# Retention with a top-k MLP on one core: decay moved from k to v, v loaded by another queue, masks split over two engines

## The chip, the core and the metric

The kernel runs on one core of a Trainium2 chip. A core has five engines that each work through a list of instructions of their own, in order: TensorE (PE: matrix products and transposes, results in PSUM), VectorE (DVE), ScalarE (ACT), GpSimd (POOL) and SyncE (SP, used here only to start transfers). DMA engines move data between memory and SBUF. Semaphores join the lists. PSUM has eight banks of 2 KB per partition; the kernel keeps one for the state and hands out the other seven.

The metric is the device time of one execution in microseconds (us), median of several. The profile is of one execution; its span is a little shorter than the time.

## The reference, cut to what matters

```python
# q, k, v: (4 batches, 8 heads, 768 positions, 64), float32
gamma = 1.0 - 2.0 ** (-5.0 - np.arange(H))             # one decay per head
state = zeros(B, H, 64, 64)
for t in range(S):
    state = gamma * state + k[:, :, t] (outer) v[:, :, t]
    y[:, :, t] = scale * (q[:, :, t] @ state)          # scale = 1/8
x = y as (B, 768, 512)                                  # heads side by side

for b in range(B):                                      # the second part
    scores = x[b] @ w_gate                              # one number per row
    top = the 128 rows of highest score
    h  = max(x[b, top] @ w1, 0)                         # 512 -> 1024
    ye = h @ w2                                         # 1024 -> 512
    out[b] = x[b];  out[b, top] += sigmoid(scores[top]) * ye
```

The recurrence is computed by chunks of 128 positions. Inside a chunk the output is (scores with a causal mask) times v; what came before is a 64 x 64 state per head. The decay between positions i and j is gamma^(i-j) = gamma^i times gamma^(-j), so one factor can be put on q and the other on k. The factor gamma^(-j) can as well be put on v: each term of the sum is a number (q_i . k_j) times the row v_j, and each term of the state is k_j times the row v_j.

## The kernel before

A block is two chunks (256 positions) of one batch; there are 12 blocks, three per batch. The file describes each step as a task with an engine, a length, a "due" and what it reads and writes. A planner inside the file orders the tasks by these numbers, and the instruction lists follow that order. The planner's numbers steer only the order; nothing waits for them on the chip. Only the parts that matter here are shown.

```python
def load(name, src, dst, t):                 # k, q, v of block t: fp32 in memory, bf16 in SBUF
    def fn(eng):
        nc.gpsimd.dma_start(dst[t]..., ap)   # all 36 loads and 8 weight loads are issued by GpSimd
    P.add(f"L{name}{t}", ("POOL", 0.8), fn, t * 3.0 - 40.0, wr=[(name, t)], dma=1.33)

# per block t
# KS: k times gamma^(-j); on VectorE for the first and last block, else on GpSimd
e.tensor_mul(ks[ring][:, r, hs, :], kx[t][:, hs, r, :], gks...)      # 4 per block, 128x256
# TK/CK: transpose ks (8 matmuls), copy PSUM -> kT (VectorE or ScalarE, in fact 10 and 2 of 12)
# TQ/CQ: transpose q (16 matmuls), qT = PSUM * gamma^i (VectorE)
# QK.j, j = 0, 1: 16 matmuls each, scores of four heads into two banks
def mk(eng, j=j, ar=ar):                     # M: the causal mask, from PSUM, fp32 -> bf16
    nc.vector.tensor_mul(am[ar]..., PS[:, ba[j].at:ba[j].at + 2, :]..., mask...)
# AV.j: am times v (16 matmuls each), QS: state times qT (4 per chunk), summed in bank by[c]
# KV: state += ks x v, 8 matmuls of 128 columns per chunk. A pair of heads shares a 128x128
#     square, of which only the two 64x64 squares on the diagonal are wanted:
def se(eng, c=c, cc=cc):                     # SE: copy only those, two operations per chunk
    for s in range(2):
        nc.scalar.activation(sn[s * 64:(s + 1) * 64, :, s * 64:(s + 1) * 64], PS[...], AF.Copy)
# per chunk: YC: xs = scale * PSUM (ScalarE), SC: scores = sum(PSUM * wg) (VectorE)

# ranking, per chunk c of a batch: RB: turn the score column into a row (matmul with identity),
# SR: copy it to SBUF, CM: compare with all earlier chunks and count (VectorE, width 128*(c+1))
# per batch (select): SP: split scores in three bf16 parts (GpSimd), CS: column sums (matmuls),
# RK, OH: one-hot rows of the 128 selected (VectorE), IG/AX/IX: their row numbers and scores,
# SG: sigmoid
# store_base: xs to out (GpSimd); fetch: gather the 128 rows from out by number
# mlp: XT (transpose), XE (copy), W1 (32 matmuls), RL (relu), W2 (8 matmuls), then
# CB (VectorE): ot = gate * W2 + rows; SS: scatter ot to out by row number (GpSimd)
```

The last batch is treated in another way: the 128 best of its first four chunks are selected, gathered and put through the MLP, and the last two chunks are put through the MLP whole ("dense"). A comparison of scores then zeroes the gate of those rows that are not among the best 128 of all six chunks.

```python
b = B - 1; NE = NC - 2
select(b, NE, e); store_base(b, NE, e - 1.0); fetch(b, e)
...                                          # counts against the scores of chunks 4 and 5
mlp(B - 1, xg[b], [("xg", b)], T1 + 1.0, 1, scatter(B - 1, b, "flc", gfl[:, 2:3]))
dense(0, j4); dense(1, j5)                   # an MLP over each of the last two chunks, plain stores
```

Of the kernel before, what the change touches and what calls it, by code (L numbers as in the profile page):

```python
# [36 lines left out]
class Task:  # L37
    __slots__ = ("name", "engs", "fn", "due", "deps", "users", "allocs", "banks", "n", "left",
                 "start", "end", "eng", "dma", "land", "idx")
# [11 lines left out]
class Plan:  # L51
# [7 lines left out]
    def add(self, name, engs, fn, due, rd=(), wr=(), alloc=(), use=(), dma=None, after=()):  # L59
# [4 lines left out]
        t.dma = dma  # L64
# [22 lines left out]
    def run(self):  # L87
# [10 lines left out]
        dma_at = 0.0  # L98
        lanes = []
# [13 lines left out]
        def place(n):  # L113
            best = None
            rng = range(self.first, self.nbanks - n + 1)
            if n == 1:
                rng = reversed(rng)
            for i in rng:
                if any(bank_held[i:i + n]):
                    continue  # L120
                f = max(bank_free[i:i + n])
                if best is None or f < best[0] - 0.05:
                    best = (f, i)
            return best

        while ready:
            cands = []
            for t in ready:
                got = 0.0
                if t.allocs:  # L130
                    held = sum(not h for h in bank_held)
                    need = sum(b.n for b in t.allocs)
                    if held - need < max(b.reserve for b in t.allocs):
                        continue
                    save_h = list(bank_held)
                    ok = True
                    for b in t.allocs:
# [5 lines left out]
                        for i in range(p[1], p[1] + b.n):  # L143
                            bank_held[i] = True
                    bank_held[:] = save_h
                    if not ok:
                        continue
                for eng, dur in t.engs:
                    s = max(free[eng], got)
                    for d in t.deps:  # L150
                        s = max(s, latency(d, eng))
                    if t.dma and len(lanes) >= 8:
                        s = max(s, lanes[-8])
                    cands.append((s, s + dur, t, eng, dur))
# [25 lines left out]
            if t.dma is not None:  # L180
                dma_at = max(dma_at, e + 0.9) + t.dma
                t.land = dma_at + 1.3
                lanes.append(t.land)
# [16 lines left out]
def kernel(  # L200
# [43 lines left out]
    kx = buf("kx", [128, H, 2, D], BF, NT)  # L244
    qx = buf("qx", [128, H, 2, D], BF, NT)
    vx = buf("vx", [128, H, 2, D], BF, NT)
    ks = buf("ks", [128, 2, H, D], BF, 3)
# [3 lines left out]
    sbd = buf("sbd", [128, HP, 128], BF, 2)  # L251
# [12 lines left out]
    gate = buf("gate", [128, 2], FT, B + 1)  # L264
# [3 lines left out]
    ot = buf("ot", [128, Dm], FT, B + 2)  # L268
    w1 = consts.tile([128, HP, F], BF, name="w1")
    w2 = consts.tile([128, FB, Dm], BF, name="w2")  # L270
    wg = consts.tile([128, Dm], FT, name="wg")
    spacer = consts.tile([1, 1], FT, name="spacer")

    P = Plan(8, 1)
    TAU = 4.6

    def load(name, src, dst, t):
        b, blk = divmod(t, NBK)
        ap = bass.AP(tensor=src.tensor, offset=src.offset + b * H * S * D + blk * 2 * C * D,
                     ap=[[2 * D, 128], [S * D, H], [1, 2 * D]])  # L280

        def fn(eng):
            nc.gpsimd.dma_start(dst[t].rearrange("p h r d -> p h (r d)"), ap)  # L283
        return P.add(f"L{name}{t}", ("POOL", 0.8), fn, t * 3.0 - 40.0, wr=[(name, t)], dma=1.33)
# [9 lines left out]
    thr = consts.tile([128, 1], FT, name="thr")  # L294
# [7 lines left out]
    gks = consts.tile([128, H, NBK * 2], FT, name="gks")  # L302

    load("k", k, kx, 0)
# [6 lines left out]
    load("q", q, qx, 0)  # L311
# [7 lines left out]
    load("v", v, vx, 0)  # L319
# [6 lines left out]
    P.add("lg", ("DVE", 0.6), c_lg, -50, wr=["lg", "ones1"])  # L326
# [5 lines left out]
    def c_gks(eng):  # L332
        for h in range(H):
            nc.scalar.activation(gks[:, h, :], pos.rearrange("p b r -> p (b r)"), AF.Exp, bias=0.0,
                                 scale=-lgam[h])
# [23 lines left out]
    def c_sbd(eng):  # L359
        for i in range(2):  # L360
            nc.vector.memset(sbd[i], 0.0)
    P.add("sbd0", ("DVE", 0.6), c_sbd, -2, wr=[("sbd", 0), ("sbd", 1)])

# [7 lines left out]
    def c_late(eng):  # L371
        nc.gpsimd.iota(slotf, pattern=[[1, 128]], base=0, channel_multiplier=0,
                       allow_small_or_imprecise_dtypes=True)
        nc.gpsimd.iota(thr, pattern=[[0, 1]], base=128, channel_multiplier=-1,
                       allow_small_or_imprecise_dtypes=True)
        nc.gpsimd.iota(tokf, pattern=[[0, 1]], base=0, channel_multiplier=2,
                       allow_small_or_imprecise_dtypes=True)
    P.add("late", ("POOL", 0.8), c_late, 9.0, wr=["slotf", "thr", "tokf"])

    def c_late2(eng):  # L380
        nc.gpsimd.tensor_copy(slots, slotf)
        nc.gpsimd.tensor_scalar(tokf[64:128], tokf[64:128], -127.0, None, op0=OP.add)
        for j in range(NCH):
            nc.gpsimd.memset(aux[:, j:j + 1, 0], float(C * j))
        nc.gpsimd.tensor_copy(aux[:, :, 1], tokf.to_broadcast([128, NCH]))
    P.add("late2", ("POOL", 3.0), c_late2, 12.0, rd=["slotf"], wr=["slots", "tokf"]
# [7 lines left out]
    for t in range(1, 3):  # L394
        load("k", k, kx, t)
        load("q", q, qx, t)
        load("v", v, vx, t)
    gq_part(1)
    gq_part(2)
    for t in range(3, NT):  # L400
        load("k", k, kx, t)
        load("q", q, qx, t)
        load("v", v, vx, t)

    def load_w(i):
        def fn(eng):
            if i < 4:
                nc.gpsimd.dma_start(w1[:, :, i * 256:(i + 1) * 256],
                                    bass.AP(tensor=moe_w1.tensor, offset=moe_w1.offset + i * 256,
                                            ap=[[F, 128], [128 * F, HP], [1, 256]]))  # L410
            else:
                f = 2 * (i - 4)
                nc.gpsimd.dma_start(w2[:, f:f + 2, :],
                                    bass.AP(tensor=moe_w2.tensor, offset=moe_w2.offset + f * 128 * Dm,
                                            ap=[[Dm, 128], [128 * Dm, 2], [1, Dm]]))
        P.add(f"W{i}", ("POOL", 0.6), fn, (4 + i * 0.25) * 3.0 - 40.0, wr=[("w", i)], dma=1.35)
    for i in range(8):
# [451 lines left out]
```

## Time and profile before

| | |
|---|---|
| time, median of 2 (lowest to highest) | 141.83 us (141.69 to 141.98) |
| span of the profiled execution | 139.8 us |
| busy: TensorE, weight loads | 100.6, 75.2 us |
| busy: VectorE, ScalarE, GpSimd | 93.9, 52.3, 87.9 us |
| mean clock granted to TensorE | 0.815 |
| DMA moved | 19.92 MB, of which 98.1% (of the transfer time) in GpSimd's queue |
| median from issue to landing of a load | 10.7 to 10.8 us |

Busy time is the sum of an engine's instructions; their shares of the span are averages over stages that differ. The profile's line for a group of instructions gives the source line, the engine, the operation, what is written and read with its shape, how many there are, then busy us and mean ns of one, and then how long the engine stood idle before them and what it waited for. A line of an engine's list in order of time gives the start and the length in us, the same description, and in brackets the idle time before it and its cause. In the rows of 40 slices each digit is the busy share of a slice in tenths (for PEclk the granted clock in tenths of full speed).

### The profile page before, as it was taken

The page shows a single profiled execution, that of the slowest core. Times are in us where ns is not written, and L with a number is a line of the kernel's source. Part 1 is how long each engine was busy: PE and PEld are TensorE (multiplying, and loading weights), DVE is VectorE, ACT ScalarE, POOL GpSimd, SP SyncE. Part 2 cuts the span into 40 slices and gives each one's busy share as a digit, 9 for nine tenths or more (in the row PEclk, how much of TensorE's full clock was granted, in tenths as well). Part 3 has the DMA queues.
Part 4 walks back from the last instruction along what each step waited for, and adds up shares of the span by engine and source line. Part 5 has one row for each costly group of instructions (what it writes and reads, how often), then busy time and mean ns, then how long its engine had stood idle before and what let it go on. Part 6 is the DMA issues. An engine that isn't in the chain of part 4 may idle for free.

```text
span 139.8 us, 3982 instructions
## 1 busy us (share of the span) xinstructions
PE 100.6 (72%) x1658; PEld 75.2 (54%) x1658; DVE 93.9 (67%) x211; ACT 52.3 (37%) x131; POOL 87.9 (63%) x187
## 2 busy tenths in 40 slices
PE   0077738987951599877968859987995989967820
PEld 0065626766730377654647559575753768645500
DVE  6467352789997162898996960799999798741130
ACT  6672512080831020736405145346541556033200
POOL 7999679999967989889999813031504471430020
PEclk9999985697797555799655555899999599999995
DMA  2999999999999999999998202010951283123012
GB/s 71 147 162 179 184 179 187 182 197 192 190 200 182 181 181 182 182 181 182 330 415 230 38 5 34 4 75 5 319 138 75 27 235 87 20 80 93 0 75 75
DMA packets 44962, 19.92 MB, mean 142 GB/s; under 512 B 37904, under 2 KB 41488, under 8 KB 44944
## 3 DMA queue, kind: packets, MB, share of 16 engines
q0 software_dynamic: 44480, 18.88, 98.1%
q1 hardware_dynamic: 304, 0.52, 1.4%
q8 instruction: 13, 0.21, 0.6%
q10 hardware_dynamic: 160, 0.26, 0.5%
q14 instruction: 5, 0.04, 0.1%
HBM read 24.38 MB, written 7.34 MB: 227 GB/s over the span
## 4 chain that ended last, share of the span: by engine, by line
PE 28%; POOL 22%; DVE 20%; DMA 16%; issue 6%; ACT 3%; ACTq 0%; POOLq 0%
POOL ks L436 8%; DMA w<-in_moe_w_dram 8%; DVE am L497 7%; DMA vx<-in_v_dram 7%; PE ps L706 7%; PE ps L724 6%; DVE gm L587 4%; PE ps L534 4%; POOL kx L283 3%; POOL qx L283 3%; PE ps L525 3%; DVE oh L626 3%; POOL vx L283 2%; PE ps L448 2%; PE ps L511 2%
## 5 line engine op out<-in xcount | busy, mean ns | idle before, releaser
L497 DVE TENSOR_TENSOR am<-ps,mask 128x1024 bf16<-128x1024 f32 x24 | 28.6, 1217 | 2.9 <-PE ps L488 2.9
L545 ACT ACTIVATE sbd<-ps 64x256 bf16<-64x256 f32 x40 | 15.1, 376 | 31.1 <-PE ps L534 21.5
L436 POOL TENSOR_TENSOR ks<-kx,gks 128x256 bf16<-128x256 bf16 x40 | 25.5, 665 | 0.2
L557 ACT ACTIVATE xs<-ps 128x512 bf16<-128x512 f32 x24 | 13.3, 595 | 15.7 <-PE ps L525 8.0
L563 DVE SCALAR_TENSOR_TENSOR scr<-ps,wg 128x512 bf16<-128x512 f32 x24 | 15.8, 685 | 3.9 <-ACT xs L557 3.9
L448 PE MATMUL ps<-ident,ks 128*128 128x128 bf16 x96 | 12.0, 263 | 8.2 <-POOL ks L436 7.9
L738 POOL DMA_INDIRECT out_dram<-ot,idx x4 | 4.1, 1023 | 21.8 <-DVE ot L733 16.9
L468 PE MATMUL ps<-ident,qx 128*64 128x128 bf16 x192 | 10.6, 276 | 9.9 <-DMA qx<-in_q_dram 9.9
L534 PE MATMUL ps<-vx,ks 64*128 64x128 bf16 x160 | 16.3, 260 | 0.7 <-ACT sbd L545 0.5
L587 DVE SCALAR_TENSOR_TENSOR gm<-srow,sc,ahead 128x128 bf16<-128x128 f32 (+5 forms) x22 | 16.3, 772 | 0.0
L511 PE MATMUL ps<-vx,am 64*128 64x64 bf16 x384 | 12.8, 210 | 4.5 <-DVE am L497 4.3
L706 PE MATMUL ps<-xgT,w 128*128 128x128 bf16 x192 | 14.3, 234 | 1.0 <-ACT xgT L695 1.0
L473 DVE TENSOR_TENSOR qT<-ps,gq 128x1024 bf16<-128x1024 bf16 x12 | 8.3, 689 | 9.5 <-PE ps L468 5.1
L468 PEld LDWEIGHTS <-qx 128*64 128x64 bf16 x192 | 8.2, 144 | 11.9 <-DMA qx<-in_q_dram 10.8
L724 PE MATMUL ps<-w,hT 128*128 128x512 bf16 x48 | 12.7, 394 | 2.5 <-ACT hT L715 2.5
L534 PEld LDWEIGHTS <-ks 64*128 64x128 bf16 x160 | 12.3, 114 | 3.5 <-issue 2.6
L706 PEld LDWEIGHTS <-w 128*128 128x128 bf16 x192 | 13.1, 106 | 1.9 <-issue 1.3
L448 PEld LDWEIGHTS <-ks 128*128 128x128 bf16 x96 | 7.7, 116 | 11.2 <-POOL ks L436 9.6
L511 PEld LDWEIGHTS <-am 64*128 64x128 bf16 x384 | 9.4, 106 | 7.7 <-DVE am L497 5.9
L488 PE MATMUL ps<-qT,kT 64*64 64x128 bf16 x384 | 11.6, 270 | 0.8 <-ACT srow L581 0.4
L283 POOL DMA_DIRECT2D kx<-in_k_dram x12 | 11.0, 917 | 1.7 <-DMA vx<-in_v_dram 0.6
L283 POOL DMA_DIRECT2D qx<-in_q_dram x12 | 10.9, 906 | 1.7 <-DMA vx<-in_v_dram 0.6
(90 smaller groups left out, 149.3 us busy)
## 6 DMA issues: line engine op xcount, KB each, us to landing
out_dram<-xs POOLq DMA_DIRECT2D x6, 768.0 KB, 6.9
kx<-in_k_dram POOLq DMA_DIRECT2D x12, 256.0 KB, 10.8
qx<-in_q_dram POOLq DMA_DIRECT2D x12, 256.0 KB, 10.7
vx<-in_v_dram POOLq DMA_DIRECT2D x12, 256.0 KB, 10.8
w<-in_moe_w_dram POOLq DMA_DIRECT2D x8, 256.0 KB, 10.7
out_dram<-xs POOLq DMA_DIRECT2D x2, 512.0 KB, 4.0
wg<-in_moe_w_gate_dram SPq DMA_DIRECT2D x1, 256.0 KB, 3.4
out_dram<-ot ACTq DMA_DIRECT2D x2, 128.0 KB, 2.6
```

What stands on the lines that cost most here:

```text
L283: nc.gpsimd.dma_start(dst[t].rearrange("p h r d -> p h (r d)"), ap)
L436: e.tensor_mul(ks[ring][:, r, hs, :], kx[t][:, hs, r, :], gks[:, hs, 2 * blk + r:2 * blk + r + 1].to_broadcast([128, 4, D]))
L448: nc.tensor.transpose(o[:, i * 128:(i + 1) * 128], ks[ring][:, r, 2 * hp:2 * hp + 2, :], ident)
L468: nc.tensor.transpose(o[s * 64:(s + 1) * 64, hp, :, r, :], qx[t][:, 2 * hp + s, r, :], ident)
L497: nc.vector.tensor_mul(am[ar].rearrange("p a r i -> p a (r i)"), PS[:, ba[j].at:ba[j].at + 2, :].rearrange("p s (a x) -> p (s a) x", a=2), ...
L511: nc.tensor.matmul(bank(by[c])[:, h * 64:(h + 1) * 64], am[ar][c * 64:(c + 1) * 64, s * 2 + hp2, r, :], vx[t][c * 64:(c + 1) * 64, h, r, : ...
L534: nc.tensor.matmul(PS[:, 0, hp * 128:(hp + 1) * 128], ks[ring][c * 64:(c + 1) * 64, r, 2 * hp:2 * hp + 2, :], vx[t][c * 64:(c + 1) * 64, 2 ...
L545: nc.scalar.activation(sn[s * 64:(s + 1) * 64, :, s * 64:(s + 1) * 64], PS[s * 64:(s + 1) * 64, 0, :].rearrange("p (a e) -> p a e", a=HP) ...
L563: nc.vector.scalar_tensor_tensor(scr[j % 2], bank(by[c]), scale, wg, op0=OP.mult, op1=OP.mult, accum_out=sc[:, j:j + 1])
L587: nc.vector.scalar_tensor_tensor(gm[c], srow[b % 2][:, :c + 1, :], sc[:, j:j + 1], ahead[:, NC - 1 - c:NC, :], op0=OP.subtract, op1=OP.is_ ...
L706: nc.tensor.matmul(bank(bh[g])[:, (f % 4) * 128:(f % 4 + 1) * 128], w1[:, d, f * 128:(f + 1) * 128], xgT[r][:, d, :], start=(d == 0), stop ...
L724: nc.tensor.matmul(bank(bp), hT[r][:, f, :], w2[:, f, :], start=(f == 0), stop=(f == FB - 1))
```

## The change

What it does, and what for:

- **The decay goes from k to v.** k and q are transposed as they were loaded, so that these steps need no scaling first. v is multiplied by gamma^(-j) instead (VS, two operations of 128x512 per block; on VectorE for block 0 and half of the last, else on GpSimd).
- **v is loaded as fp32 by SyncE**, into four buffers that are used in turn; the multiplication also makes it bf16. SyncE's load of block t+4 waits for the multiplication of block t. For the first four blocks a small write by GpSimd (gate_v) ahead of each load sets when it may start. k and q still go through GpSimd; those of the third and fourth batch are loaded three blocks at a time, and the weights in four pieces for eight.
- **Half of the scores are first copied by ScalarE** to SBUF in bf16 and then masked there by VectorE; the other half is masked out of PSUM as before. The copy of kT is always ScalarE's.
- **The state is built by products of 64 columns**, only the squares that are wanted, into a bank that is zeroed once, so that one operation of 128x512 copies it.
- **The two chunks of an output are copied in one operation**; their banks are a pair.
- **No dense MLP.** The last batch is ranked over all six chunks like the others. Its rows are not gathered from memory but picked out of SBUF by matmuls with the one-hot rows (GT gives them transposed, GR as they are).
- **The other batches' MLP ends** in a scaling on ScalarE and an addition on GpSimd, not in one operation on VectorE.
- **The planner** gets earliest times for loads (REL, RELW), other due times, two transfer queues in its model, and a rule for PSUM banks that keeps pairs together.

```diff
-    TAU = 4.6
+    TAU = 6.0
+    WB = 6.5
+    REL = [0, 0, 0, 0, 12, 16, 20, 0, 0, 44]
+    RELW = [34, 36, 38, 40]
+    VIA_ACT = {(t, 1) for t in range(NT)}
+    MD = 40.0
 ...
+    def load_v(t):
+        if t < len(vf):
+            def gate_v(eng):
+                nc.gpsimd.memset(vf[t][:1, 0, 0, :1], 0.0)
+            P.add(f"GV{t}", ("POOL", 0.1), gate_v, t * 4.0 - 40.0, wr=[("v", t)])
         def fn(eng):
-            nc.gpsimd.dma_start(dst[t].rearrange("p h r d -> p h (r d)"), ap)
+            nc.sync.dma_start(vf[t % 4].rearrange("p h r d -> p h (r d)"), ap)
 ...
+    for t, n in ((1, 1), (2, 1), (3, 1), (4, 1), (5, 1), (6, 3), (9, 3)):
+        load("k", k, kxa, t, n)
+        load("q", q, qxa, t, n)
 ...
-                    e.tensor_mul(ks[ring][:, r, hs, :], kx[t][:, hs, r, :], ...)
-            P.add(f"KS{t}.{g}", [("DVE", 0.7)] if edge else [("POOL", 1.3)], fn, T0 - 6.0 + 0.1 * g,
+                e.tensor_mul(vx[ring][:, hs]..., vf[t % 4][:, hs]..., gks[:, blk, hs, :]...)
+            P.add(f"VS{t}.{g}", [("DVE", 0.7)] if t == 0 or (last and g) else [("POOL", 1.33)], fn,
 ...
-            P.add(f"M{t}.{j}", ("DVE", 1.2), mk, T0 + 0.2 * j, rd=["mask"], wr=[("am", ar)],
+            if (t, j) in VIA_ACT:
+                def ac(eng, j=j, amv=amv, pav=pav):
+                    nc.scalar.activation(amv, pav(j), AF.Copy)
+                P.add(f"AC{t}.{j}", ("ACT", 1.04), ac, T0 + 0.2 * j, wr=[("am", ar)], use=[ba[j]])
+                def mk(eng, amv=amv, mkv=mkv):
+                    nc.vector.tensor_mul(amv, amv, mkv)
+                P.add(f"M{t}.{j}", ("DVE", 0.62), mk, T0 + 0.3 + 0.2 * j, rd=["mask"], wr=[("am", ar)])
 ...
                 def se(eng, c=c, cc=cc):
-                    for s in range(2):
-                        nc.scalar.activation(sn[s * 64:(s + 1) * 64, :, s * 64:(s + 1) * 64], ...)
+                    nc.scalar.activation(st[(cc + 1) % 2]..., PS[:, 0, :], AF.Copy)
 ...
+        if last:                     # the last batch's rows: picked by one-hot matmuls out of xs
+            GT{g}: nc.tensor.matmul(bank(bt)..., xs[:, m * NC + c, ...], oh[m % 2][:, c, :], ...)
+            GR:    nc.tensor.matmul(bank(br), oh[m % 2][:, c, :], xs[:, m * NC + c, :], ...)
+            XR:    nc.scalar.activation(xg[m], bank(br), AF.Copy)
 ...
-    dense(0, j4)
-    dense(1, j5)
```

(Cuts are marked by "..."; the three lines GT, GR and XR are shortened.)

## The prediction

> **What bounds the kernel now.** I read the page first, its 40 slices above all, then the in-order lists of GpSimd, VectorE and TensorE, then the waits, and last the groups by line. No engine is full over the whole span, so the bound has to be read by stage.
>
> The slices (each is 3.5 us; I count them from 0):
>
> ```profile
> span 139.8 us, 3982 instructions
> ...
> DVE  6467352789997162898996960799999798741130
> ACT  6672512080831020736405145346541556033200
> POOL 7999679999967989889999813031504471430020
> PEclk9999985697797555799655555899999599999995
> DMA  2999999999999999999998202010951283123012
> ```
>
> The reader is to see three stages. Up to slice 19 (about 66 us) the DMA engines and GpSimd are full while VectorE has holes (3, 5, 2 in slices 4 to 6; 1, 6, 2 in 13 to 15). In slices 19 to 27 VectorE is mostly full, and TensorE has half its clock in six of them. From slice 34 (119 us) on nothing is full: that is a chain of waits.
>
> Stage 1 is explained by GpSimd's list, here around the fifth block (t=4):
>
> ```profile
> 42.27 0.87 POOL L283 DMA_DIRECT2D kx<-in_k_dram  x1 [0.41 <-DMA w<-in_moe_w_dram]
> 43.59 0.87 POOL L283 DMA_DIRECT2D qx<-in_q_dram  x1 [0.45 <-DMA w<-in_moe_w_dram]
> 44.48 1.21 POOL L436 TENSOR_TENSOR ks<-kx,gks 128x256 bf16<-128x256 bf16 x2
> ```
>
> The k of block 4 was issued at 14.60 us and a load takes at most 11.4 us to land (the loads' own line), so it was there at 26 us. Its scaling ran at 44.48, because GpSimd runs in order and eighteen issues of later blocks and weights stood ahead, some waiting for a landing. VectorE's list gives the result: the first masked score product of blocks 0 to 11 starts at 11.6, 24.9, 30.9, 36.7, 50.8, 59.0, 67.8, 76.8, 91.7, 98.0, 104.6, 110.8. An undisturbed step is 6 us (24.9 to 36.7); steps 0-1 and 3-4 lose 7 and 8 us to GpSimd, and step 7-8 loses about 8 us to the first MLP on a TensorE at half clock.
>
> Stage 3 in TensorE's list:
>
> ```profile
> 124.86 1.95 PE L706 MATMUL ps<-xgT,w 128*128 128x128 bf16 x32 [0.69 <-ACT xgT L695]
> 127.85 1.04 PE L724 MATMUL ps<-w,hT 128*128 128x512 bf16 x4 [1.04 <-ACT hT L715]
> 128.72 1.95 PE L706 MATMUL ps<-xgT,w 128*128 128x128 bf16 x32
> 130.53 1.90 PE L724 MATMUL ps<-w,hT 128*128 128x512 bf16 x8
> 133.18 1.04 PE L724 MATMUL ps<-w,hT 128*128 128x512 bf16 x4 [0.75 <-ACT hT L715]
> ```
>
> These are whole MLPs after the last score (118.0 us): the selected rows of the last batch and two dense ones, one behind another. From 118.0 to 139.8 is 21.8 us.
>
> The rows that price the work:
>
> ```profile
> L497 DVE TENSOR_TENSOR am<-ps,mask 128x1024 bf16<-128x1024 f32 x24 | 28.6, 1217 | 2.9 <-PE ps L488 2.9
> L436 POOL TENSOR_TENSOR ks<-kx,gks 128x256 bf16<-128x256 bf16 x40 | 25.5, 665 | 0.2
> L473 DVE TENSOR_TENSOR qT<-ps,gq 128x1024 bf16<-128x1024 bf16 x12 | 8.3, 689 | 9.5 <-PE ps L468 5.1
> ```
>
> **What the Trainium skill says.**
> 1. "SBUF — State Buffer", § Who interferes with whom: a VectorE instruction with two SBUF inputs, or in a two-port mode, contends with a GpSimd instruction that reads SBUF. The trace agrees: the 768-wide comparison took 2.72 us at 69.6 us beside GpSimd's scaling, 1.01 us at 39.8 without it.
> 2. "DMA: Bandwidth & Descriptors", § Issuing engines are not separate DMA queues: loads issued by SyncE and GpSimd run on the same 16 DMA engines and interleave. No run here shows two streams of loads yet. I take it that v through SyncE is no new bandwidth.
> 3. "VectorE: DVE Perf Modes", § The perf-mode tier table: a two-input operation on bf16 in SBUF runs at twice the fp32 rate, and any PSUM operand stops that. The trace disagrees on the second half: L473 reads bf16 from PSUM at 689 ns per 1024, L497 fp32 from PSUM at 1217. I price the new SBUF mask as 0.69.
> 4. "TensorE: Matmul & The Clock Gate", § What's actually happening: the clock is full or half, by TensorE's recent activity. The trace shows both values; from 78 to 84 us it was 0.50 with TensorE busy 4.12 of 6.00 us.
>
> **The change part by part.** I go along the path that sets the end: first mask, ninth step, last score, tail.
>
> *VectorE per block.* Before: two masks 2.43, qT 0.69, kT copy 0.69 (10 of 12), two scores 1.37, two comparisons 1.36 (from 0.34, 0.48, 0.61, 0.74, 0.88, 1.02 undisturbed: 4.07 per batch of three blocks), one-hot rows 1.42 per batch = 0.47. Sum 7.0. After: the kT copy goes to ScalarE and one mask of two becomes 0.69: 7.0 - 0.69 - 0.53 = 5.8. The disturbances by GpSimd cost 2.72 - 1.01 and 2.59 - 1.02 in the two worst cases, 3.3 us over 12 blocks, say 0.3 each, and the new mask is one more operation that can be hit: 6.2.
>
> *ScalarE per block.* kT 1.02 (as its row of two has it), scores 1.02 (taken as the same), state copy 0.60 x 20/12 = 1.0 (before 0.39 x 2 x 20/12 = 1.3), output 1.02 in one, two score rows 0.55: 4.6. Under VectorE's 6.2, so beside it.
>
> *GpSimd.* The 40 scalings of 256 elements, 25.5 us, become 21 of 512 elements in fp32; at 624 ns median per 256 that is 1.25 each, 26 us. Nothing saved, but the order changes: in the instruction order of the changed kernel the decay of block 4 stands directly behind that of block 3 and ahead of every weight load, and v of block t+4 is issued by SyncE. So steps 0-1 and 3-4 should lose their 15 us.
>
> *TensorE per block at full clock.* q transposes 0.57, k the same (before 0.54), scores 0.65, their product with v 0.68, state 16 x 2 smaller matmuls for 8 x 2, about 0.9 (before 1.1), output from state 0.45, rows 0.35: 4.2. Equal within what I can tell.
>
> *First mask.* k, q and v of block 0 now arrive together, and two decays of 0.6 us stand ahead of it on VectorE: 13.0 instead of 11.6.
>
> *To block 9.* Two floors. VectorE: 13.0 + 9 x 6.2 = 69. Data: a load of 256 KB (262,144 bytes) at some 181 GB/s is 1.45 us. Ahead of the last q stand 36 loads and the weights of eight: 44 x 1.45 = 63.8, and the store of batch 0, 1.57 MB at about 410 GB/s (what slices 19-20 reach), 3.8. The first q landed at 7.85 after two loads, so a start of 4.95: 4.95 + 67.6 = 72.5. q transpose, qT and scores add 2.0: block 9 at 74.5. I price v in fp32 like k because it has as many packets; that is an estimate. The data floor is the later: 75, against 98.0.
>
> *Block 9 to the last score.* Before 20.0 us. After, TensorE has three blocks (12.6) and two MLPs (1.8 + 1.9 + 0.3 each, 8.0): 20.6, VectorE about 19. I take 21: last score at 96.
>
> *Tail.* Row transpose 0.32, copy 0.28, comparison 1.1, column sums 0.54, rank 0.16, one-hot 1.25, last gather matmuls 0.4, copy 0.6, W1 1.95, relu 0.6, second half of W2 1.04, combine 0.75, gap to the scatter 0.73 (as at 123.0), scatter to landing 2.8, end 0.8, some twelve handovers of 0.05: 13.9. The MLP of batch 2 runs in its gaps; I add 1: 15, against 21.8. The two dense MLPs (7.6 us of TensorE) go, and a chain through the full ranking of six chunks comes back.
>
> Sum: 96 + 15 = 111 of span. The times lie 2.0 above the span (141.83 and 139.8): 113. One microsecond for waits that no floor has: **114**.
>
> **The rivals.**
> *TensorE at half clock is the bound.* Then a block costs 2 x 4.2 = 8.4, block 9 comes at 13 + 76 = 89, and the three last blocks at a mean clock of 0.75 take 27: 89 + 27 + 15 + 2 = 133. For it: 66 to 98 us ran at 0.68. Against: in the stage where VectorE was kept fed (98 to 118) the clock was 0.91. Half of this would give 123.
> *GpSimd stays the bound.* It still issues k, q and weights and waits for landings, and a decay is a single piece of 1.25 us. If steps 0-1 and 3-4 lose as before, block 9 comes at 88 and the time is 127. The order speaks against it.
> *Data arrive later.* v in a stream of its own runs up to four blocks ahead and takes a share from k and q; weights are issued late, so engines may idle and then be short. 5 to 8 us: 119 to 122.
> *The masks through ScalarE only move the wait.* VectorE, in order, would then wait for the copy. 0.5 us in each of 12 blocks: 120.
> *All removed waits are hidden.* Then the tail alone gains: 135. I see nothing for it.
>
> **Range and chances.** All rivals but the last cost 5 to 20 us and none is likely alone; two small ones at once give 126. If the weights load faster than I price them and TensorE stays warm, block 9 comes at 70 and the time is 105. Range 105 to 127. Slower than 139 would take several rivals at once: faster 0.94, same 0.04, slower 0.02.
>
> **What would show each step.** Masks of blocks 1 and 4 starting under 7 us after the ones before; GpSimd without waits on DMA up to block 4; block 9's mask at 75 with q waited for just before; the SBUF mask at 0.6 to 0.7 us; last score near 96; 15 us behind it. It is wrong if the mean clock falls under 0.75 before 75 us, or if VectorE's waits are for ScalarE.

## The result and the profile after

The changed kernel takes 125.34 us (124.59 to 126.1) against 141.83 before: ratio 0.8838, 95% interval 0.8606 to 0.9069. The prediction was 114 in a range of 105 to 127. The direction and the range hold; the point is 11 us too low, and most of this part is about those 11 us.

The same rows of the page as were shown of before; a slice is now 3.1 us:

```profile
span 122.8 us, 4329 instructions
...
DVE  5242616295098898839838999899598928871020
ACT  7739561434364953894555655489458087725500
POOL 7992799659303699499537969545305713786630
PEclk9999999999999996557859555589999999999998
DMA  2999999999999999999999999999910239712102
```

The holes of VectorE have not gone: they lie in slices 1 to 10 (3 to 34 us), and GpSimd has holes there too (2 in slice 3, 3, 0 and 3 in slices 10 to 12). So GpSimd is no longer what VectorE waits for. The row that stays at 9 is DMA, up to slice 28 (89 us), where before it fell at slice 22 (77 us).

The waits of the engines between 8 and 36 us (columns: us in total, times, longest):

```profile
PE ps L499 <- DMA kxa<-in_k_dram: 10.2, 4, 5.7
DVE qT L521 <- PE ps L515: 10.7, 3, 4.0
...
PE ps L515 <- DMA qxa<-in_q_dram: 2.8, 4, 1.6
```

TensorE waits for k and q (L499 is TK, L515 is TQ), and VectorE for TensorE. TensorE's list shows where (start, duration, and the wait before in brackets; L536 is QK):

```profile
21.81 1.06 PE L499 MATMUL ps<-ident,kxa 128*64 128x128 bf16 x16 [2.96 <-DMA kxa<-in_k_dram]
...
25.45 1.06 PE L515 MATMUL ps<-ident,qxa 128*64 128x128 bf16 x16 [0.21 <-DMA qxa<-in_q_dram]
...
29.69 1.06 PE L499 MATMUL ps<-ident,kxa 128*64 128x128 bf16 x16 [1.24 <-DMA kxa<-in_k_dram]
32.37 1.06 PE L515 MATMUL ps<-ident,qxa 128*64 128x128 bf16 x16 [1.62 <-DMA qxa<-in_q_dram]
...
33.77 1.08 PE L536 MATMUL ps<-qT,kT 64*64 64x128 bf16 x30
```

The k of block 2 comes at 21.8, k and q of block 3 at 29.7 and 32.4. As the list is in order, the scores of block 1 stand behind the first of these waits and those of block 2 behind the other two. The chain of work that ended last (start, us, what) has one wait for a load, the q of block 3, issued at 8.98 us:

```profile
8.98 23.34 DMA qxa<-in_q_dram
...
32.37 1.08 PE ps L515 x10
```

From there on it runs over the engines alone, and after 36 us no engine is shown waiting for k, q or v. The page's rows of the loads say why k and q are late (the last column is the median from issue to landing, us):

```profile
vf<-in_v_dram SPq DMA_DIRECT2D x12, 512.0 KB, 11.9
...
kxa<-in_k_dram POOLq DMA_DIRECT2D x6, 256.0 KB, 18.7
qxa<-in_q_dram POOLq DMA_DIRECT2D x6, 256.0 KB, 19.4
```

A k load took 10.7 us in the kernel before. It now takes 18.7, although the load itself is the same.

The start of the first mask (L556) of some blocks, of the last score, and the end, in us, for the kernel before, the one after, and the runs of the next section whose order can be compared (spans are of the profiled execution, times the median of all):

| run | block 0 | 1 | 2 | 3 | 9 | last score | end of span | time |
|---|---|---|---|---|---|---|---|---|
| before | 11.6 | 24.9 | 30.9 | 36.7 | 98.0 | 118.0 | 139.8 | 141.83 |
| after | 13.0 | 23.9 | 35.3 | 38.3 | 87.7 | 106.1 | 122.8 | 125.34 |
| predicted | 13.0 | | | | 75 | 96 | 111 | 114 |
| e2_v_few | 12.6 | 23.3 | 33.9 | 36.9 | 83.5 | 101.8 | 118.6 | 120.39 |
| e6_qk_first | 12.9 | 20.6 | 30.8 | 36.2 | 87.1 | 104.5 | 121.3 | 122.99 |
| e7_v_bf16 | 12.2 | 21.3 | 28.4 | 34.4 | 78.5 | 95.9 | 112.6 | 114.45 |
| e9_all_few2 | 14.7 | 22.4 | 32.6 | 36.3 | 80.4 | 97.8 | 115.0 | 116.82 |
| e10_v_fp32_pool | 12.8 | 21.1 | 27.9 | 33.9 | 78.7 | 96.2 | 112.8 | 115.24 |
| e11_v_two | 13.6 | 20.9 | 28.7 | 33.2 | 87.0 | 104.8 | 121.6 | 123.34 |
| e12_v_gated | 12.6 | 21.9 | 33.8 | 36.8 | 86.3 | 103.7 | 120.4 | 122.07 |

How far two profiles of the same work differ shows in e8_gr_late, whose lists are those of after up to the tail: 14.9, 25.7, 36.4, 39.3 and 88.0 in these columns, where after has 13.0, 23.9, 35.3, 38.3 and 87.7. A difference of 1 to 2 us in one column alone says little.

So the first mask came when predicted, block 9 came 12.7 us late, block 9 to the last score was faster than predicted (18.4 against 21) and the tail slower (16.7 against 15).

### The profile page after: what moved, and what is told of

Same layout as the page of the kernel before. It is cut to its first block, busy times and chain, and to the rows that moved or that the text cites. A ratio compares the mean times of both kernels' runs of the same rounds, so it can differ in the third digit from the quotient of the medians.

```text
span 122.8 us, 4329 instructions
## 1 busy us (share of the span) xinstructions
PE 90.4 (74%) x1862; PEld 69.3 (56%) x1866; DVE 78.0 (64%) x189; ACT 68.2 (56%) x119; POOL 75.6 (62%) x129
## 4 chain that ended last, share of the span: by engine, by line
PE 35%; DMA 19%; DVE 15%; issue 10%; POOL 9%; ACT 8%; POOLq 1%; ACTq 0%
DMA qxa<-in_q_dram 19%; PE ps L600 5%; PE ps L567 5%; PE ps L515 5%; PE ps L499 4%; PE ps L626 4%; DVE scr L613 4%; ACT xs L607 4%; PE ps L583 4%; PE ps L536 3%; POOL kxa L320 3%; DVE am L556 3%; DVE oh L676 3%; ACT am L548 3%; PE ps L785 2%
## 5 line engine op out<-in xcount | busy, mean ns | idle before, releaser
L482 POOL TENSOR_TENSOR vx<-vf,gks 128x512 bf16<-128x512 f32 x21 | 22.9, 1108 | 12.5 <-PE ps L567 9.1
L499 PE MATMUL ps<-ident,kxa 128*64 128x128 bf16 x192 | 11.2, 284 | 11.7 <-DMA kxa<-in_k_dram 10.2
L556 DVE TENSOR_TENSOR am<-ps,mask 128x1024 bf16<-128x1024 f32 x12 | 14.6, 1221 | 5.5 <-PE ps L536 5.5
L505 ACT ACTIVATE kT<-ps 128x1024 bf16<-128x1024 bf16 x12 | 12.3, 1022 | 10.6 <-PE ps L499 10.6
L521 DVE TENSOR_TENSOR qT<-ps,gq 128x1024 bf16<-128x1024 bf16 x12 | 8.2, 688 | 14.7 <-PE ps L515 14.7
L607 ACT ACTIVATE xs<-ps 128x1024 bf16<-128x1024 f32 x12 | 12.3, 1023 | 7.6 <-PE ps L600 7.6
L593 ACT ACTIVATE st<-ps 128x512 bf16<-128x512 f32 x20 | 12.0, 598 | 7.9 <-PE ps L583 5.6
L499 PEld LDWEIGHTS <-kxa 128*64 128x64 bf16 x192 | 8.5, 148 | 13.8 <-DMA kxa<-in_k_dram 11.1
L536 PE MATMUL ps<-qT,kT 64*64 64x128 bf16 x384 | 13.7, 280 | 1.4 <-DVE qT L521 0.9
L583 PE MATMUL ps<-vx,kxa 64*64 64x64 bf16 x320 | 11.4, 218 | 3.9 <-issue 2.7
L548 ACT ACTIVATE am<-ps 128x1024 bf16<-128x1024 f32 x12 | 12.3, 1022 | 3.5 <-PE ps L536 3.5
L515 PE MATMUL ps<-ident,qxa 128*64 128x128 bf16 x192 | 10.0, 268 | 2.8 <-DMA qxa<-in_q_dram 2.8
L536 PEld LDWEIGHTS <-kT 64*64 64x64 bf16 x384 | 9.5, 141 | 3.6 <-issue 3.2
L515 PEld LDWEIGHTS <-qxa 128*64 128x64 bf16 x192 | 7.9, 140 | 4.6 <-DMA qxa<-in_q_dram 3.8
L600 PE MATMUL ps<-st,qT 128*128 128x128 bf16 x80 | 9.6, 283 | 0.5 <-issue 0.5
## 6 DMA issues: line engine op xcount, KB each, us to landing
kxa<-in_k_dram POOLq DMA_DIRECT2D x6, 256.0 KB, 18.7
```

The lines of the kernel that those rows point to most:

```text
L482: e.tensor_mul(vx[ring][:, hs].rearrange("p h r d -> p (h r) d"), vf[t % 4][:, hs].rearrange("p h r d -> p (h r) d"), gks[:, blk, hs, :].r ...
L499: nc.tensor.transpose(o[s * 64:(s + 1) * 64, hp, r, :], kx[t][:, 2 * hp + s, r, :], ident)
L515: nc.tensor.transpose(o[s * 64:(s + 1) * 64, hp, :, r, :], qx[t][:, 2 * hp + s, r, :], ident)
L536: nc.tensor.matmul(bank(ba[j], s)[c * 64:(c + 1) * 64, (hp2 * 2 + r) * 128:(hp2 * 2 + r + 1) * 128], kT[ring][s * 64:(s + 1) * 64, hp, r, ...
L548: nc.scalar.activation(amv, pav(j), AF.Copy)
L556: nc.vector.tensor_mul(amv, pav(j), mkv)
```

## The experiments

Two theories stood at the start. *Data theory*: k and q land late because v shares the DMA engines with them. *Engine theory*: VectorE, GpSimd and their order set the pace, and the waits for data only fill time that would be lost anyway.

**e1_load_price: what a load costs.** A kernel with loads only, in four phases of eight loads. It leaves out the whole computation.

```diff
+    # 1: v as fp32 by SyncE, alone        2: v as bf16 by GpSimd, alone
+    # 3: v as fp32 by SyncE beside k as bf16 by GpSimd        4: v as fp32 by GpSimd, alone
+    for i in range(N):
+        nc.sync.dma_start(vf[i], ap(v, i))
+    for i in range(N):
+        nc.gpsimd.tensor_copy(vb[i][:1, 0, :1], vf[i][:1, 0, :1])   # marks the landing
```

> The disputed cost by itself: nothing but loads of eight blocks, in four phases, each after the one before: v as fp32 by SyncE; the same v as bf16 by GpSimd; v as fp32 by SyncE and k as bf16 by GpSimd at the same time; v as fp32 by GpSimd. The rest of the computation is left out. Data theory (an fp32 load costs the DMA engines more than a bf16 one): 2.2 to 2.3 us a load in phase 1 against 1.4 to 1.5 in phase 2, phase 3 about 3.7 us for a pair, phase 4 like phase 1. Theory of the prediction (a load is priced by its 1,024 packets): 1.45 in phases 1, 2 and 4, 2.9 for a pair. Third possibility (only the mixing of two queues costs): 1.45 in phases 1 and 2, 3.7 for a pair in phase 3.

GpSimd's list; each row is a copy of one element that waits for one load, so the distance of two rows is the price of a load. Two rows each of phase 1, of phase 2, of the time in which bf16 loads run beside fp32 loads, and of phase 4:

```profile
12.27 0.18 POOL L43 CAST vb<-vf 1x1 bf16<-1x1 f32 x1 [1.62 <-DMA vf<-in_v_dram]
14.07 0.18 POOL L43 CAST vb<-vf 1x1 bf16<-1x1 f32 x1 [1.62 <-DMA vf<-in_v_dram]
...
27.70 0.17 POOL L48 CAST vf<-vb 1x1 f32<-1x1 bf16 x1 [1.27 <-DMA vb<-in_v_dram]
29.15 0.17 POOL L48 CAST vf<-vb 1x1 f32<-1x1 bf16 x1 [1.27 <-DMA vb<-in_v_dram]
...
36.05 0.17 POOL L48 CAST vf<-vb 1x1 f32<-1x1 bf16 x1 [3.50 <-DMA vb<-in_v_dram]
39.78 0.17 POOL L48 CAST vf<-vb 1x1 f32<-1x1 bf16 x1 [3.55 <-DMA vb<-in_v_dram]
...
74.19 0.17 POOL L61 COPY zz<-vg 1x1 f32<-1x1 f32 x1 [1.63 <-DMA vg<-in_v_dram]
76.00 0.18 POOL L61 COPY zz<-vg 1x1 f32<-1x1 f32 x1 [1.64 <-DMA vg<-in_v_dram]
```

In bf16 a load costs 1.45 us, in fp32 1.81, from either engine. With two queues at work a bf16 load lands every 3.69 us, and an fp32 load beside it: more than 1.45 + 1.81 = 3.26, and for the queue of k and q 2.5 times as long as alone. This is the number that the prediction lacked. None of the three expectations had 1.81; two had the 3.7 of a pair. The Trainium skill has the rule, "DMA: Bandwidth & Descriptors", § Queues, rings and completion order: a DMA engine goes round the queues that have work, packet by packet. The measured pace agrees: one load of one queue, one of the other, however many wait in either.

**e2_v_few: little v after block 3.** Blocks 4 to 11 load one head of v instead of eight; the other heads are left from earlier blocks.

```diff
-            nc.sync.dma_start(vf[t % 4]..., ap)
+            if t < 4: nc.sync.dma_start(vf[t % 4]..., ap)
+            else: nc.sync.dma_start(vf[t % 4][:, :1]..., few)     # one head
```

> The changed kernel, but the loads of v for blocks 4 to 11 bring one head of eight (the other heads stay those of earlier blocks, so this part of the data is left out); every engine's list is the same. Data theory: some 16 us of transfers go, most of what ran beside the first k and q; block 2's first mask comes at 26 to 29 us instead of 35.3, block 9's at 78 to 80 instead of 87.7, time 115 to 118. Engine theory (VectorE, with its lock against GpSimd, and TensorE's clock set the pace and late data are made up for later): block 2 comes earlier but block 9 at 84 or later, time 122 to 125.

120.39 us, ratio 0.8441 (0.8381 to 0.8501): 5 us less than after, and with block 9 at 83.5 between what the two theories had. But block 2's mask stayed at 33.9, since v of blocks 0 to 3 is still whole and k2 still came at 21.2. What v costs before 35 us must then come from its first loads, which e11 tests.

**e3_decay_few: little decay on GpSimd.** 8 of 64 columns of v are decayed; the other columns of vx are left from before.

```diff
-                e.tensor_mul(vx[...], vf[...], gks[...])
+                n = 8 if eng == "POOL" else D
+                e.tensor_mul(vx[...][:, :, :n], vf[...][:, :, :n], gks[...])
```

> The changed kernel, but GpSimd's multiplications of v work on 8 of 64 columns (the rest of v is left out), so that GpSimd hardly reads SBUF and cannot hold VectorE up; lists as before but for two fillings at the start. Engine theory: the stretched comparisons and one-hot rows (6 to 7 us in the sum of VectorE) fall back to their own length and the time falls by 5 to 7 us. Data theory: the first 35 us stay, and as VectorE then has slack the time falls by 0 to 3 us.

125.33 us, ratio 0.8836 (0.8804 to 0.8867): nothing. The decay fell from 1108 ns to 299 ns, 17 us of GpSimd's work in all, and block 9's mask stood at 87.69 as before. GpSimd's work and its disturbance of VectorE are off the path in this kernel.

**e4_mask_direct: both masks by VectorE from PSUM.** The copy by ScalarE and the mask in SBUF are replaced by one mask of 1.22 us at the place of the copy.

```diff
-                    nc.scalar.activation(amv, pav(j), AF.Copy)
+                    nc.vector.tensor_mul(amv, pav(j), mkv0)
```

> The changed kernel with one part undone: the second half of the scores is masked straight out of PSUM by VectorE, at the place of ScalarE's copy. VectorE gets 12 x 0.53 = 6.4 us more work, ScalarE 12.3 us less. Engine theory: VectorE is the pace after block 2, so ten blocks x 0.53: 4 to 6 us slower. Data theory: 0 to 3 us slower. If the copy through ScalarE only moves the wait: no change or faster.

125.37 us, ratio 0.882 (0.878 to 0.8861): not to be told from after, and the 4 to 6 us of engine theory did not come. This part of the change can be taken back without a loss that these runs show, as long as data come late. (The profiled execution, 126.95 us, was disturbed, so only the times are used; the other three have a median of 125.03.)

**e5_all_few: no data for blocks 2 to 11, first try.** All loads of k and q from block 2 on shrink to one head, written into a spare tile; these blocks work on the k and q of blocks 0 and 1.

```diff
+    kx = [kxa[0][:, :, t % 2] for t in range(NT)]      # the same for qx
+        if t >= 2:
+            to = few                                   # one spare tile for all
```

> Blocks 2 to 11 get no data of their own: k and q of blocks 2 to 11 are loaded as one head into a spare tile that nothing waits for, and these blocks work on the k and q of blocks 0 and 1; v of blocks 4 to 11 is one head. All instructions of the engines stay, in their order. Data theory (k and q that land late set the pace up to block 9): block 2's first mask at 25 to 28 instead of 35.3, block 9's at 68 to 72 instead of 87.7, last score at 87 to 91, end at 104 to 108. TensorE-order theory (only the 5.8 us that the transposes of blocks 2 and 3 wait for k and q go, and from block 3 on the engines pass the work to each other as slowly as before): block 2 at 28 to 30, block 9 at 79 to 82, last score at 97 to 100, end at 114 to 117.

127.87 us, slower than with all data. The edit made a wait of its own. GpSimd's waits between 8 and 60 us begin with:

```profile
POOL few L325 <- DMA few<-in_k_dram: 19.5, 5, 11.2
```

As all shrunk loads write one tile, each had to wait until the one before had landed. The run says nothing of the two theories.

**e6_qk_first: scores ahead of later transposes.** TensorE's and VectorE's lists are rearranged, nothing else.

```diff
+    move("TK2", after="QK1.1"); move("CK2", after="TK2")
+    move("TK3", after="QK2.0"); move("TQ3", after="TK3"); move("CK3", after="TK3")
+    move("CQ3", after="TQ3")    # with SC2, SC3 and M2.0 ahead of it
```

> In TensorE's list the scores of block 1 go ahead of the k transposes of block 2, and the first half of block 2's scores (with the first mask and block 1's gating scores on VectorE) ahead of the transposes of block 3. Data theory and order theory agree on the masks: block 1's first mask at 20 to 21 instead of 23.9, block 2's at 28 to 29 instead of 35.3. If waiting behind later blocks' transposes is what costs (order theory), block 3 follows at 35 to 36 instead of 38.3 and the end comes 2 to 4 us earlier, at about 122 us. If the data rate sets the pace (data theory), block 4 stands where it was (49 to 50) and the end moves by less than 1 us.

122.99 us, ratio 0.8684 (0.8613 to 0.8754). Blocks 1, 2 and 3 came 3.4, 4.5 and 2.0 us earlier, block 4 only 0.7 (48.9 against 49.6), block 9 only 0.6. What the order gains early is given back by block 4. The 2.4 us of the time lie within the interval of the run after, so this experiment doesn't tell a gain from none.

**e7_v_bf16: v cast in its load, in the queue of k and q.** GpSimd issues v; the decay stays where it is.

```diff
-    vf = buf("vf", [128, H, 2, D], FT, 4)
+    vf = buf("vf", [128, H, 2, D], BF, NT)
-            nc.sync.dma_start(vf[t % 4]..., ap)
+            nc.gpsimd.dma_start(vf[t]..., ap)
+    move("Lv4", after="Lq3")
```

> v is cast to bf16 in its load and issued by GpSimd like k and q, into a buffer of its own per block; the decay stays on GpSimd. One queue carries all: 36 loads of 256 KB written at the 1.45 us measured for such loads alone, instead of 3.69 us for a pair of k or q and v in two queues plus 1.45. That is 36 x 1.45 = 52.2 us against 12 x 3.69 + 12 x 1.45 = 61.7 us. Data theory: block 2's first mask 5 to 6 us earlier (9 loads have to be there: 9 x 1.45 + 7 = 20 for q2, 24.5 for q3), block 9's about 8 us earlier, end at 116 to 119. Theory that two queues share by turns and the price of fp32 are of no account beside the engines' order: the end within 1.5 us of 125.3.

114.45 us, ratio 0.8099 (0.8036 to 0.8162): 10.9 us less than after, and more than data theory asked. After 8 us no transpose waits for data any more. The run changes three things at once, the type, the queue and the order of issue.

**e10_v_fp32_pool: the type put back.** v is fp32 again, in GpSimd's queue at the same places.

```diff
+    vf = buf("vf", [128, H, 2, D], FT, 10)
+            nc.gpsimd.dma_start(vf[t % 10]..., ap)
```

> v stays fp32, decayed from fp32, but is issued by GpSimd at the same places as in e7_v_bf16 (114.45), so that one queue carries all loads in the order in which they are issued; 10 buffers, none waited for. If fp32 itself is the cost (1.81 instead of 1.45 us a load, 12 x 0.36 = 4.3 us in all, 1.1 us up to q2, 1.4 up to q3): between 115.5 and 118.5. If the second queue is the cost (turns with k and q, v running ahead): 114.5 to 117, with block 2's first mask at 28.5 to 30. If v in fp32 is costly in another way (its traffic slows the engines, or its decay from fp32 does): 121 or more, block 2 past 32.

115.24 us, ratio 0.8172 (0.8123 to 0.8221). The type is worth some 0.8 us, and the intervals of the two runs overlap. The loads' rows of this run:

```profile
vf<-in_v_dram POOLq DMA_DIRECT2D x12, 512.0 KB, 11.0
...
kxa<-in_k_dram POOLq DMA_DIRECT2D x6, 256.0 KB, 8.4
qxa<-in_q_dram POOLq DMA_DIRECT2D x6, 256.0 KB, 9.9
```

and its TensorE at the place shown above of after:

```profile
18.96 1.06 PE L499 MATMUL ps<-ident,kxa 128*64 128x128 bf16 x16
...
22.17 0.64 PE L515 MATMUL ps<-ident,qxa 128*64 128x128 bf16 x16
...
24.97 0.64 PE L499 MATMUL ps<-ident,kxa 128*64 128x128 bf16 x16
25.44 0.61 PE L515 MATMUL ps<-ident,qxa 128*64 128x128 bf16 x16
```

The same four transposes that stood at 21.8, 25.5, 29.7 and 32.4, none of them waiting. The same 22.9 MB are moved, but k lands after 8.4 us instead of 18.7, because it queues behind the v that was issued before it and not beside v that was issued after it.

**e12_v_gated: only the queue put back.** As e10, but SyncE issues v, each load released by GpSimd at the place where it issued the load in e10.

```diff
-            nc.gpsimd.dma_start(vf[t % 10]..., ap)
+            nc.gpsimd.memset(vf[t % 10][:1, 0, 0, :1], 0.0)
+            nc.sync.dma_start(vf[t % 10]..., ap)
```

> The run with v in fp32 in GpSimd's queue (e10_v_fp32_pool, 115.24) with one thing put back: v is issued by SyncE into its own queue again, each load released by a one-element write of GpSimd at the place where GpSimd issued it; order, 10 buffers and type stay. Queue theory (v in a second queue takes turns with k and q packet by packet, so it gets its share before k and q that are older): k2 and q2 late again, block 1's first mask at 22 to 24.5, block 2's at 31 to 35.5, block 9's at 84 to 88, end at 121 to 125.5. Theory that e10's gain came from the order of issue or from the buffers, which allow v to be issued without waiting: block 2 at 27.5 to 29.5, end at 114 to 117.

122.07 us, ratio 0.8633 (0.8562 to 0.8705), as queue theory has it: 6.8 us more than e10, with intervals that don't meet. Its TensorE:

```profile
19.81 1.06 PE L500 MATMUL ps<-ident,kxa 128*64 128x128 bf16 x16 [0.55 <-DMA kxa<-in_k_dram]
23.54 1.07 PE L516 MATMUL ps<-ident,qxa 128*64 128x128 bf16 x16 [0.29 <-DMA qxa<-in_q_dram]
27.18 1.07 PE L500 MATMUL ps<-ident,kxa 128*64 128x128 bf16 x16 [0.64 <-DMA kxa<-in_k_dram]
30.91 1.07 PE L516 MATMUL ps<-ident,qxa 128*64 128x128 bf16 x16 [2.66 <-DMA qxa<-in_q_dram]
```

The second queue alone makes the transpose of block 3's q late by 5.5 us (30.91 against 25.44). The remaining 3.3 us up to after (125.34) belong to order and buffers: there v4 is issued ahead of v3, and k2 comes at 21.8 instead of 19.8. The interval of after is too wide to call these 3 us sure. One rival was not run: the page calls GpSimd's queue software_dynamic and SyncE's hardware_dynamic, so whether two queues of the same kind would take turns in this way stays open.

**e11_v_two: v can't run ahead.** SyncE keeps v, but with two buffers, so that a load waits for the decay of the block two before.

```diff
-    vf = buf("vf", [128, H, 2, D], FT, 4)
+    vf = buf("vf", [128, H, 2, D], FT, 2)
+    move("Lv3", after="VS1.1")     # and so on: Lv{t} after VS{t-2}.1
```

> v stays fp32 in SyncE's queue, but with two buffers: the load of a block is issued only when the block two before it has been decayed, so v can no longer run four blocks ahead. Run-ahead theory (early v loads take turns with k and q that are needed sooner): k2 lands at 18 to 19 instead of 21.8, block 1's first mask at 20.5 to 22, block 2's at 30 to 32, end at 120.5 to 122.5. Theory that only the amount counts: the end stays within 1 us of 125.3. Should v itself come too late (a load issued, landed and decayed takes longer than two blocks of 6 us): slower, 127 to 130, with GpSimd's decay waiting for v.

123.34 us, ratio 0.8665 (0.859 to 0.874). Two effects are in it. Up to block 3 the run is as early as e10 (28.7 and 33.2): v that runs ahead is what takes the share from k and q there. Later v is late itself. How long the instructions on v's tile (the decay, L483, 19.5 us of it on GpSimd) waited for its loads, in us and times:

```profile
  DMA vf<-in_v_dram: 21.1, 7
```

Two of these loads, 9.2 and 13.0 us long, lie between block 1 and block 9 on the chain that ended last, and block 9 stands at 87.0, close to after.

**e9_all_few2: no data for blocks 2 to 11, a spare tile for each load.**

```diff
-            to = few
+            to = few[f"{name}{t}"]
```

> As e5_all_few (blocks 2 to 11 work on the k and q of blocks 0 and 1, v of blocks 4 to 11 is one head), but every shrunk load goes into a spare tile of its own, so that no load waits for the one before. Data theory: with k and q there at once, block 2's first mask at 25 to 29, block 9's at 72 to 78, the end at 106 to 112, no later than the run with v in bf16 (112.6). Order theory: the engines' lists set the pace from block 3 on as before, block 2 at 28 to 30, block 9 at 79 to 82, the end at 114 to 117.

116.82 us (one run), with block 2 at 32.6: later than in e10, which loads everything. Both theories missed this. Block 9 (80.4) and the end are where order theory had them, and e7 and e10 are no slower than this run that hardly loads k and q: so late data can no longer set much of their time. From the first mask of block 1 to that of block 2 e9 needs 10.2 us and e10 6.9, and no data are waited for in this stretch. Two things differ. A comparison (L647 here, 128 wide) on VectorE beside GpSimd's decay:

```profile
23.99 2.72 DVE L647 SCALAR_TENSOR_TENSOR gm<-srow,sc,ahead 128x128 bf16<-128x128 f32 x1
```

In e10 it took 1.9 us less:

```profile
22.49 0.84 DVE L637 SCALAR_TENSOR_TENSOR gm<-srow,sc,ahead 128x128 bf16<-128x128 f32 x1
```

And TensorE in e9:

```profile
28.89 1.06 PE L509 MATMUL ps<-ident,kxa 128*64 128x128 bf16 x16
29.74 1.01 PE L525 MATMUL ps<-ident,qxa 128*64 128x128 bf16 x16
```

Transposes at 1.06 and 1.01 where e10 shows 0.64 and 0.61; with the product and the outputs before them (0.61 + 1.04 against 0.41 + 0.62) that is 1.4. 1.9 + 1.4 is the whole 3.3 us. "TensorE: Matmul & The Clock Gate", § What's actually happening, of the Trainium skill has it: the array runs at half its clock until it has been busy for some time, and again after idling.

The row PEclk stands at 9 there, but it has nothing to show: the trace of each run has the clock from its first change on, and the row fills the time before with 9. The first record, a change to full speed, lies at 21.9 us in e10, 26.3 in e11, 30.6 in e9, 39.3 in e12 and 40.0 in after, and just there the instructions become short. Where the clock is recorded, row and transposes agree. In e10 TensorE later waited 2.4 us for a mask and was slow again behind it:

```profile
32.05 0.54 PE L567 MATMUL ps<-vx,am 64*128 64x64 bf16 x16 [2.37 <-DVE am L552]
...
34.48 1.07 PE L515 MATMUL ps<-ident,qxa 128*64 128x128 bf16 x16
```

and its row falls in slices 11 and 12 (31 to 37 us):

```profile
PEclk9999999999976999679995555599999999999996
```

These lines agree with the page. So a wait can cost twice: its own length, and a slow TensorE for what follows. The last wait ahead of e9's slow transposes was 2.1 us for a mask, not for data; no run sets the two costs apart.

**e8_gr_late: the tail.** The six matmuls that gather the last batch's rows (L754) go behind W1.

```diff
+    move("GR", after="W1.3.3")
+    move("XR", after="RL3.1")
```

> In the tail, the six matmuls that gather the last batch's rows go behind the third quarter of its first MLP product instead of ahead of it, and the copy that needs them behind the last relu. Reading of the tail: these six stood for 1.46 us in front of a product whose operand was ready 1.1 us earlier, so the last product, and the end, come 1.0 to 1.3 us earlier, all else the same (124.2 us). If something else in the tail ends later (the scatter, the gate), nothing moves (125.3).

124.23 us, ratio 0.8774 (0.8693 to 0.8854), not to be told from after; from the last score to the end it is 16.9 us against 16.7. The move put the six in front of the next step of the chain:

```profile
111.56 1.95 PE L785 MATMUL ps<-xgT,w 128*128 128x128 bf16 x32
113.34 1.46 PE L754 MATMUL ps<-xs,oh 128*128 128x512 bf16 x6
114.64 1.89 PE L803 MATMUL ps<-w,hT 128*128 128x512 bf16 x8
```

The first half of hT was ready at 113.31 (ScalarE's list), but W2 (L803) started at 114.64. What W1 gained, W2 lost.

## Why the prediction was right in its range and 11 us off

*First mask: right, with some luck.* 13.0 predicted, 13.03 measured; runs with the same beginning have it between 12.6 (e2) and 14.9 (e8).

*Steps 0-1 and 3-4 "should lose their 15 us" to GpSimd: half right.* GpSimd doesn't hold VectorE any more, and block 1 to block 9 fell from 73.1 to 63.8 us. But the two steps still take 10.9 and 11.4 us. In the first TensorE waits for k; the second is mostly VectorE's own work (below). The sign that I named, under 7 us, did not come. The 15 us were too much from the start: in these two steps, 13.2 and 14.1 us long before the change, VectorE was idle for 6.3 and 4.9 us. (Step 7-8 lost 8.9 us, not about 8.)

*"Data floor" 74.5: this step failed.* Its sum takes all loads as one queue, each after those issued before it, at 1.45 us. The price of fp32 in it was wrong (1.81), yet that costs only some 0.8 us (e7 against e10). Wrong was the order: with v in a queue of its own the k and q loads go on at one per 3.69 us as long as any v waits, whatever the age of either. I had this as a rival at 119 to 122 ("takes a share from k and q") and gave it little; it is the main part of the 11 us. e12 against e10 shows 6.8 us of it with type, order and buffers unchanged. The floor also looked for the wait in the wrong place: it is at blocks 1 to 3, where TensorE waits for k and q of blocks 2 and 3, and not at block 9.

How well the sum itself was priced is seen where v is in the same queue. GB/s of the DMA engines from 55 us to 95 us, one number a microsecond, first of e7:

```profile
GB/s 206 209 179 200 205 195 181 182 189 181 183 182 183 183 195 200 290 405 416 383 422 389 403 365 176 107 53 16 0 0 0 0 0 262 31 112 5 403 354 289
```

and of after:

```profile
GB/s 279 262 241 203 215 216 216 216 218 221 208 218 216 213 215 201 197 179 182 182 182 183 196 199 282 350 402 404 418 403 393 360 205 181 67 2 0 16 0 0
```

Loads cast to bf16 show as some 182; the stores behind them as 400. The last q of e7 landed at 72.5 us (issued at 53.75, landed 18.8 later), where I had it, that of after at 81.5 (57.43 + 24.1).

*From the last q to block 9's mask, 2.0 us: too small, and not what held it.* In e7 it is 78.5 - 72.5, in after 87.7 - 81.5, 6.0 to 6.2: TensorE's list has the transposes of three blocks, k and q, and state and row work ahead of block 9's scores. I counted one block's. And the sign that I named, this q waited for, came in neither run: TensorE went to the first of these transposes straight from other work, at 79.93 in after and at 72.25 in e7.

*VectorE at 6.2 us a block: of no account in after.* e3 and e4 change its disturbance or its work and the time stays; they were not repeated on e10. But 6.2 is the mean of unlike blocks. In the step from block 3 to block 4, with the end of batch 0's ranking in it, VectorE is busy 9.8 of 11.4 us in after and 9.8 of 10.0 in e10: there it is the floor or close to it, and a step under 7 us could not come. Its parts were sized well. The masks of after:

```profile
L556 DVE TENSOR_TENSOR am<-ps,mask 128x1024 bf16<-128x1024 f32 x12 | 14.6, 1221 | 5.5 <-PE ps L536 5.5
L552 DVE TENSOR_TENSOR am<-am,mask 128x1024 bf16<-128x1024 bf16 x12 | 8.7, 724 | 0.9 <-ACT am L548 0.8
```

0.72 on average against the 0.69 that I took, and 0.8 us of waits for ScalarE's copy in the whole kernel: the rival "masks through ScalarE only move the wait" falls.

*TensorE at half clock: a part, and not by the row that I watched.* The row has nothing of the first 40.0 us of after. With these counted at half, the mean up to 75 us is an estimated 0.6 (0.86 by the row less 0.5 x 40 / 75), under the 0.75 that I had named as a sign of being wrong; but in e10 it is an estimated 0.7 (0.86 less 0.5 x 21.9 / 75), so this sign tells little. After block 3 the clock doesn't set the pace: up to block 9 e7 takes 44.1 us at a mean of 0.68, e12 49.5 at 0.79. Before, it accounts for 1.4 us in the one stretch where I could set two runs side by side; its share in all of after was not isolated.

*Block 9 to the last score: 18.4 for 21; tail: 16.7 for 15.* These cancel nearly. Of the tail, the gathering matmuls (L743) took 1.50 us where I put 0.4, and from the scatter's issue (118.23) to the end it is 4.6 instead of 3.6.

So 114 was the time of a kernel that has v in the queue of k and q: e7 ran in 114.45. Even there block 9 came 3.5 us later than predicted and the way to the last score 3.6 us faster, so part of that agreement is luck.

*What stays open.* After block 3, e12 loses another 4.6 us to e10 (from the first mask of block 3 to the last score 66.9 against 62.3). Its transposes wait 2.2 us for k and q there. TensorE also stands still for 4.5 us (1.7 in e10) at four places for which the profile names nothing that it waits for ("issue"). One of them, in e12 and in e10:

```profile
65.14 0.41 PE L584 MATMUL ps<-vx,kxa 64*64 64x64 bf16 x14 [1.82 <-issue]
```

```profile
58.49 0.41 PE L583 MATMUL ps<-vx,kxa 64*64 64x64 bf16 x14 [1.28 <-issue]
```

The same places cost 4.2 us in after, 0.7 in e7, and are not listed in e9, which loads least. That they have to do with the loads is likely; what TensorE waits for there isn't recorded, and no run isolates it. A TensorE kept busy during the early waits was not tried.

## What to carry to other kernels

A second DMA queue was no second road here: it took every other turn, so a stream that wasn't needed yet went past one that was. Put loads that are consumed together into one queue in the order of their use. Holding the second queue back did not replace that: a gate at the place where e10 issues v left 122.07 us (e12), and two buffers left 123.34, as v then came late itself (e11). When you price a floor from bytes, ask which load goes first, and look at which block the data are waited for. When a wait is on TensorE, count the slow TensorE behind it too, and read it from the lengths of like instructions, since PEclk shows nothing before its first change.

## What the runs showed of the hardware that I had not expected

- Two queues of loads together were slower than one: a bf16 and an fp32 load of 1,024 rows take 3.69 us side by side and 1.45 + 1.81 = 3.26 one after another.
- fp32 without a cast is moved faster in bytes (0.52 MB in 1.81 us, 290 GB/s written) than the cast to bf16 (0.26 MB in 1.45 us, 181 GB/s), but slower per load.
- TensorE starts slow and can stay so for long: 16 transposes took 1.06 us instead of 0.64 up to 22 us in one order of loads (e10) and up to 40 us in another (after). PEclk reads 9 all this time, because it has no record before its first change.
- A 128-wide comparison on VectorE took 0.34 us in after and 2.72 us in e9, beside GpSimd's decay.
